# VectorE's share of the exps as fp16 bits: a chain of six passes in place of seven, an offset carried by an added row of Q and K, and new rules for the order of instructions

## The chip, the cores and the metric

One core of a Trainium2 chip. The metric is the device time of one execution in microseconds (us), lower is better. A result is the median of several runs; a verdict calls two kernels the same within 2%. Ratios are the mean time of one kernel's fast runs over that of the other's fast runs of the same rounds, so they are not quite the ratio of the medians quoted beside them.

## The reference

Two independent parts are computed and concatenated. Part A is a spectral filter (a 2-D FFT, a product with complex weights, the inverse FFT) on 2048 x 640. Part B, which the change concerns, is full attention with 32 heads of 20 columns over 2048 positions:

```python
qkv = (x @ wqkv).reshape(B, S, 3, H, Dh).transpose(2, 0, 3, 1, 4)   # H = 32, Dh = 20, S = 2048
scores = einsum("bhqd,bhkd->bhqk", q, k) * Dh ** -0.5
p = softmax(scores, axis=-1)
o = einsum("bhqk,bhkd->bhqd", p, v)
b = o.transpose(0, 2, 1, 3).reshape(B, S, D) @ wo
```

## The kernel before

The kernel cuts attention into 32 units (four blocks of 512 queries by eight groups of four heads). A unit has 64 tiles of 128 keys by 512 queries. TensorE makes the scores of two or three tiles into a half of PSUM. ScalarE takes the exp of that half in one instruction, and TensorE sums the result against V, four heads side by side, into one PSUM bank. A column of ones in V yields the softmax's denominator. Part A's matmuls and evictions are laid between.

ScalarE alone would need longer than the rest, so VectorE computes 238 of the 2048 tiles by itself, two tiles at a time. It turns the score into the bits of a floating-point number and corrects the mantissa with a polynomial:

```python
# first, for each of two tiles, from PSUM (128x512, fp32 -> uint16)
v = score * (1024 * SCALE * LOG2E) + (32 * 1024 + 512)
# then on both together (128x1024, 16 bit), seven passes
sh  = v << 6                                        # step 0  cheap pass
t   = sh * (X_K / 65536) + X_K * X_BETA             # step 1  cheap pass
h   = t * t                                         # step 2  tensor_tensor
t   = t * (X_GAMMA / X_K) + (1 - X_GAMMA * X_BETA)  # step 3  cheap pass
h   = h * t                                         # step 4  tensor_tensor
v   = v + h                                         # step 5  tensor_tensor
v   = v * 0.125 + X_BIAS                            # step 6  cheap pass: now the bits of a bf16
```

No engine's program is written by hand. While the kernel is built, a list scheduler plays it through with a cost per instruction and appends each instruction to its engine's queue when the engine and the inputs are free in that play. On the chip each engine then works its queue strictly in order, and waits by semaphore. So a wrong cost puts instructions in an order in which one engine stands behind another. Three of its rules (cut):

```python
# the weighted sum with V goes when tiles of four heads are ready, or what is left of the unit
if len(pick) < min(least, self.pv_left[u]):       # least = 4
    return False
...
# the unit's end: denominators go out by DMA, come back broadcast over partitions, then normalize
self.dma(rb, src, r=[("rs", u)], w=[("rb",)], ...)
self.dve_urgent.append((self.now + 3600.0, lambda: self.unit_norm(u), ...))
...
# a filler matmul that adds zero, when TensorE's recent share is under WARM_SHARE
if self.share() > self.cfg["WARM_SHARE"]: return False
```

The sums are checked at the end. If they lie outside a certified range, a slow and safe version runs afterwards. With these inputs it never does.

## Time and profile before

| | before |
|---|---|
| median, range | 921.6 us, 921.09 to 927.94 (3 runs) |
| span of the profiled run | 915.7 us |
| ScalarE, VectorE, TensorE busy | 839.7, 815.7, 837.9 us |
| exps on ScalarE: count, busy, idle before them | 724, 828.8 us, 53.4 us |
| VectorE idle before normalize | 15.9 us |
| mean granted TensorE clock | 0.963 of full |

Read "idle before them" as the holes in ScalarE's row of exps. The prediction shows the page's groups and the instructions around two holes. One row of the page is needed besides: the granted TensorE clock in 40 slices of the span, in tenths of full speed.

```profile
PEclk9999999999699999999999998999799999679999
```

Five slices dip (6, 8, 7, 6, 7). Windows of half a microsecond read 0.50 inside the dips and 1.00 outside them, with mixed values only where a dip starts or ends. So the clock has two states here, and a mean of 0.963 means that 2 x 0.037 x 915.7 = 68 us of the span ran at half.

### The profile page before, as it was taken

How to read it: one execution, taken by the hardware profiler on the slowest of the kernel's cores; microseconds unless marked ns; L12 is line 12 of the kernel's file. 1: busy time of each engine (PE TensorE's matmuls, PEld its weight loads, DVE VectorE, ACT ScalarE, POOL GpSimd, SP SyncE). 2: the span in 40 equal slices, each digit the busy share in tenths (PEclk: the TensorE clock that was granted, in tenths of full speed). 3: DMA queues.
4: the chain of work that ended last, by engine and by line, in shares of the span. 5: the costliest groups of instructions: out<-in, count | busy, mean ns of one | idle time of the engine just before them, and what ended most of it. 6: DMA issues, size and time to landing. Idle time of an engine off the chain costs nothing.

```text
span 915.7 us, 16468 instructions
## 1 busy us (share of the span) xinstructions
PE 837.9 (92%) x6731; PEld 291.2 (32%) x6823; DVE 815.7 (89%) x1642; ACT 839.7 (92%) x744; POOL 2.9 (0%) x7
## 2 busy tenths in 40 slices
PE   8999999999899999999999997898899998989986
PEld 4433333333233333322233322223233332223222
DVE  5797799999799998999899999999999898678994
ACT  6898999998799999999999995999799999789993
POOL 1000000000000000000000000000000000000000
PEclk9999999999699999999999998999799999679999
DMA  7430000003200000011001000010010201011100
GB/s 228 87 82 14 2 14 13 14 14 93 73 28 27 13 14 13 14 48 36 13 20 35 13 13 1 13 59 14 1 59 20 78 13 42 1 41 43 42 13 32
DMA packets 31830, 31.85 MB, mean 35 GB/s; under 512 B 13444, under 2 KB 26500, under 8 KB 31492
## 3 DMA queue, kind: packets, MB, share of 16 engines
q1 hardware_dynamic: 31748, 30.73, 11.2%
q8 instruction: 55, 0.90, 0.4%
q14 instruction: 27, 0.22, 0.1%
HBM read 24.97 MB, written 5.50 MB: 33 GB/s over the span
## 4 chain that ended last, share of the span: by engine, by line
ACT 52%; PE 21%; DVE 20%; DMA 5%; issue 1%; SPq 0%; ACTq 0%; DVEq 0%
ACT arena L1714 51%; PE ps L1697 6%; DVE arena L227 4%; DMA arena<-rscr 4%; PE ps L1879 4%; DVE arena L1787 3%; DVE arena L1253 2%; PE ps L1331 2%; DVE arena L1828 1%; DVE arena L1835 1%; DVE arena L1832 1%; PE ps L1596 1%; DVE arena L1258 1%; PE ps L1533 1%; PE ps L1583 1%
## 5 line engine op out<-in xcount | busy, mean ns | idle before, releaser
L1714 ACT ACTIVATE arena<-ps 128x1536 bf16<-128x1536 f32 x724 | 828.8, 1276 | 53.4 <-PE ps L1697 28.2
L1697 PE MATMUL ps<-arena 32*128 32x512 bf16 x2048 | 309.3, 394 | 42.4 <-ACT arena L1714 22.5
L1879 PE MATMUL ps<-arena 128*32 128x512 bf16 (+1 forms) x2048 | 208.3, 401 | 5.0 <-DVE arena L1837 2.2
L1787 DVE TENSOR_SCALAR arena<-ps 128x512 uint16<-128x512 f32 x238 | 163.4, 687 | 30.6 <-PE ps L1697 28.4
L227 DVE CAST arena<-ps 128x512 bf16<-128x512 f32 (+4 forms) x248 | 143.7, 580 | 22.6 <-PE ps L1331 6.1
L1697 PEld LDWEIGHTS ps<-arena 32*128 32x128 bf16 x2048 | 74.3, 91 | 247.9 <-ACT arena L1714 180.7
L1879 PEld LDWEIGHTS ps<-arena 128*32 128x32 bf16 (+1 forms) x2048 | 51.3, 92 | 132.4 <-issue 107.6
L1583 PE MATMUL ps<-arena 128*128 128x512 bf16 x244 | 85.3, 397 | 3.5 <-issue 2.4
L1828 DVE TENSOR_TENSOR arena<-arena 128x1024 f16<-128x1024 f16 x119 | 81.8, 687 | 1.1
L1832 DVE TENSOR_TENSOR arena<-arena 128x1024 f16<-128x1024 f16 x119 | 81.9, 688 | 0.9
L1835 DVE TENSOR_TENSOR arena<-arena 128x1024 uint16<-128x1024 uint16 x119 | 81.5, 685 | 0.6
L1826 DVE TENSOR_SCALAR arena<-arena 128x1024 f16<-128x1024 int16 x119 | 50.4, 424 | 0.8
L1830 DVE TENSOR_SCALAR arena<-arena 128x1024 f16<-128x1024 f16 x119 | 50.1, 421 | 0.9
L1824 DVE TENSOR_SCALAR arena<-arena 128x1024 uint16<-128x1024 uint16 x119 | 50.1, 422 | 0.4
L1837 DVE TENSOR_SCALAR arena<-arena 128x1024 uint16<-128x1024 uint16 x119 | 50.1, 421 | 0.4
L1533 PE MATMUL ps<-arena 128*32 128x512 bf16 x640 | 47.8, 381 | 1.2 <-issue 0.5
L1596 PE MATMUL ps<-arena 128*128 128x512 bf16 x145 | 46.5, 396 | 1.5 <-issue 0.8
L1331 PE MATMUL ps<-arena 128*128 128x320 bf16 (+1 forms) x192 | 43.0, 330 | 4.3 <-DVE arena L1787 4.2
L227 DVE COPY arena<-ps 128x1024 bf16<-128x1024 bf16 (+2 forms) x55 | 40.2, 733 | 6.0 <-PE ps L540 4.6
L1583 PEld LDWEIGHTS ps<-arena 128*128 128x128 bf16 x317 | 26.7, 98 | 44.9 <-issue 39.3
L1964 PE MATMUL ps<-arena 128*128 128x320 bf16 x192 | 38.2, 303 | 0.1
L1942 DVE TENSOR_TENSOR arena<-arena 128x512 bf16<-128x512 f32 x31 | 21.4, 689 | 15.9 <-DMA arena<-rscr 15.4
(71 smaller groups left out, 464.3 us busy)
## 6 DMA issues: line engine op xcount, KB each, us to landing
arena<-rscr SPq DMA_DIRECT2D x31, 256.0 KB
arena<-in_B_x_dram SPq DMA_DIRECT2D x4, 640.0 KB, 6.4
arena<-in_A_x_dram SPq DMA_DIRECT2D x4, 640.0 KB, 6.2
out_dram<-arena SPq DMA_DIRECT2D x16, 160.0 KB, 1.8
out_dram<-arena SPq DMA_DIRECT2D x4, 640.0 KB, 3.4
arena<-f_ciCS SPq DMA_DIRECT2D x2, 1024.0 KB, 5.1
arena<-arena SPq DMA_DIRECT2D x124, 2.0 KB, 1.7
arena<-f_cslab SPq DMA_DIRECT2D x2, 768.0 KB, 4.4
```

Source lines behind the costliest of these rows:

```text
L227: return eng.tensor_copy(out, in_)
L1331: return lambda e: e.matmul(o, l, r_, start=s_, stop=e_)
L1533: inst = e.matmul(ps[32 * j:32 * j + 32, bank, :], self.wqkv[:, cbv, c:c + 32], r_, start=st, stop=sp, tile_position=(0, 32 * j))
L1583: self.P.add("pe", lambda e: e.matmul(ps[:, 6, :], z, k[:, 0, 0:512], start=False, stop=False, skip_group_check=True), r=[("KT", 0, 0), (" ...
L1596: return lambda e: e.matmul(o, l, r_, start=st, stop=sp)
L1697: inst = e.matmul(ps[:, bank, :], kt_[32 * j:32 * j + 32, g, kt * 128:(kt + 1) * 128], q[32 * j:32 * j + 32, :], start=True, stop=True, ti ...
L1714: self.P.add("act", lambda e: e.activation(pt, in_, AF.Exp, scale=SCALE), r=[("ps", h + k) for k in range(n)], w=[("PT", i % 4)], name="exp")
L1787: self.P.add("dve", lambda e: e.tensor_scalar(v, in_, 1024.0 * SCALE * LOG2E, 32.0 * 1024 + 512, ALU.mult, ALU.add), r=[("ps", bank)], **( ...
L1828: t = self.x_op(n, two, lambda e: e.tensor_tensor(h16, t16, t16, ALU.mult), [ka], [kb], "x_q")
L1832: t = self.x_op(n, two, lambda e: e.tensor_tensor(h16, h16, t16, ALU.mult), [ka, kb], [kb], "x_h")
L1835: t = self.x_op(n, two, lambda e: e.tensor_tensor(v, v, h16, ALU.add), [kb, kv], [kv], "x_w")
L1879: inst = e.matmul(ps[32 * j:32 * j + m, 6, :], va[:, kt, 21 * h:21 * h + m], pt, start=st, stop=sp, tile_position=(0, 32 * j))
```

## The change

The intent is to drop the last pass. If the added constant makes 15, the exponent bias of fp16, part of the score itself, the first instruction's bits are already those of fp16 and need no rescaling. So a row is added to Q (46.5) and to K (1.0) in the padding of the 32-row tile, which adds 46.5 to every score; 46.5 x 0.2236 = 15 x ln 2. ScalarE takes the same amount off by an immediate bias in its exp. With it come new scheduling rules: normalize is placed 9.0 us after the broadcast's issue, part A's multiplications and strided copies get truer costs, the weighted sum may go with fewer heads when ScalarE is stuck, and several weights change. The core of the diff:

```diff
-  activation(pt, in_, AF.Exp, scale=SCALE)
+  activation(pt, in_, AF.Exp, scale=SCALE, bias=-15.0 / LOG2E)
-  v = tensor_scalar(score, 1024.0 * SCALE * LOG2E, 32.0 * 1024 + 512, ALU.mult, ALU.add)
+  v = tensor_scalar(score, 1024.0 * SCALE * LOG2E, 31743.0, ALU.mult, ALU.min)
   (six passes remain: shift, a line, sh * line, a second line, product, add to v)
-  elif step == 6:
-      t = self.x_op(n, one, lambda e: e.tensor_scalar(v, v, 0.125, X_BIAS, ALU.mult, ALU.add), ...)
   # evictions of Q and K: a plain copy becomes multiply and add by a [128,1] operand each
+  return e.tensor_scalar(out, in_, m, b, ALU.mult, ALU.add)
   # two reductions of the sums per unit become one (cut)
   ...
-  if len(pick) < min(least, self.pv_left[u]):
+  stuck = (next exp's scores are ready, its output buffer isn't free, ScalarE is idle)      # shortened
+  if len(pick) < (1 if stuck else min(least, heads)):
-  self.dve_urgent.append((self.now + 3600.0, ... unit_norm ...))
+  self.dve_urgent.append((self.now + self.cfg["T_RB"], ... unit_norm ...))                  # 9000
-  costs: 1.0417 * ne + 64 (multiply, combine); 0.52 * n (copy); eviction + 40
+  costs: 1.0417 * ne + 124, + 144;             1.0417 * n for the strided copy; eviction + 3 on VectorE
-  T_A=680000.0, WIN=1000.0, T_X=0.0
+  T_A=760000.0, WIN=1400.0, T_X=40000.0, T_RB=9000.0
```

More of the change, by code (lines that the diff above doesn't have):

```diff
@@ L1122, in mkev @@
                         return lambda e, en: copy_on(e, en, o, in_)
-                    ev = [(mkev, 0.833 * n * 128 + 63, 0.52 * n * 128 + 64, [], [dst_key(c, b0 // 8)] + zwr, [])]
+                    ev = [(mkev, 0.833 * n * 128 + 63, (1.0417 if tag == "UT" else 0.52) * n * 128 + 64, [], [dst_key(c, b0 // 8)] + zwr, [])]
                     aft = after[c] if isinstance(after, dict) else after
@@ L1253, in mkev @@
                     return lambda e, en: e.tensor_tensor(t[k], ps[:, bank, 0:ne], w, ALU.mult)
-                return (mkev, 0.0, 1.0417 * ne + 64, kw, [("tmp", k)] + zw("K", 2), [])
+                return (mkev, 0.0, 1.0417 * ne + 124, kw, [("tmp", k)] + zw("K", 2), [])
             def comb(y, k0, k1, op, key, t=t):
@@ L1258, in mkev @@
                     return lambda e, en: e.tensor_tensor(y, t[k0], t[k1], op)
-                return (mkev, 0.0, 1.0417 * ne + 64, [("tmp", k0), ("tmp", k1), zr("K", 2)], [key] + zw("B", 3), [])
+                return (mkev, 0.0, 1.0417 * ne + 144, [("tmp", k0), ("tmp", k1), zr("K", 2)], [key] + zw("B", 3), [])
             for co in range(2):
@@ L1370 @@
 LOG2E = 1.4426950408889634
-X_K, X_BETA, X_GAMMA = 18.8641107, -0.0282624809, 0.224521806
-X_BIAS = 12084.9708
+Y_ROW = 46.5
+X_A, X_B = 0.30457565, 0.07826797
 MODE = 100.0
 SLACK = 200.0
+F16 = mybir.dt.float16
 DMA_NS = 2200.0
@@ L1415, in alloc @@
         self.outB = [a.bf(take(1280), 640) for _ in range(2)]
-        self.rin = a.f32(take(64), 16)
-        self.rc = a.f32(take(64), 16)
+        self.rr = a.f32(take(128), 32)
+        self.rin, self.rc = self.rr[:, 0:16], self.rr[:, 16:32]
+        self.kq = a.f32(take(32), 8)
         self.mm = a.f32(take(256), 64)
         self.cert = a.f32(take(32), 8)
-        self.flagt = a.f32(take(32), 8)
+        self.flagt = self.cert[:, 6:8]
         self.vmx = a.f32(take(64), 16)
@@ L1462, in setup_B @@
         self.dma(self.ident, cBd.ap(), w=[("ident",)], name="ld_ident")
+        kq = np.zeros((128, 8), np.float32)
+        kq[:, 0] = kq[:, 2] = 1.0
+        kq[20::32, 0:4] = (0.0, 1.0, 0.0, Y_ROW)
+        kqd = self.nc.inline_tensor(kq, self.prefix + "kq")
+        self.dma(self.kq, kqd.ap(), w=[("kq",)], name="ld_kq")
         xB = self.B_x[0].rearrange("(t p) c -> p t c", p=128)
@@ L1492, in setup_B, with add_row @@
         self.wpad("act", 0)
+    def add_row(self, e, en, out, in_, c):
+        m, b = self.kq[:, c:c + 1], self.kq[:, c + 1:c + 2]
+        if en == "act":
+            return e.activation(out, in_, AF.Identity, bias=b, scale=m)
+        return e.tensor_scalar(out, in_, m, b, ALU.mult, ALU.add)
     def wpad(self, en, g):
@@ L1539, in mk_jobs_B_static, with mkev @@
                 J.pe = pe
+                def mkev(bank, g=g, kc=kc):
+                    o = self.KT[:, g, kc * 512:(kc + 1) * 512]
+                    return lambda e, en: self.add_row(e, en, o, ps[:, bank, :], 0)
+                J.ev = [(mkev, 490.0, 600.0, [("kq",)], [("KT", g, kc)], [])]
                 J.mode = "c"
@@ L1600, in mkev @@
             o = self.QA[u % 2]
-            in_ = ps[:, bank, :]
-            return lambda e, en: copy_on(e, en, o, in_)
-        ev = [(mkev, 490.0, 598.0, [], [("QA", u % 2)], [])]
+            return lambda e, en: self.add_row(e, en, o, ps[:, bank, :], 2)
+        ev = [(mkev, 490.0, 600.0, [("kq",)], [("QA", u % 2)], [])]
         cond = lambda p: g in self.wq_done and (u < 2 or self.qk_left[u - 2] == 0)
@@ L1713, in try_exp @@
         in_ = self.ps[:, h:h + n, :].rearrange("p b n -> p (b n)")
-        self.P.add("act", lambda e: e.activation(pt, in_, AF.Exp, scale=SCALE),
+        self.P.add("act", lambda e: e.activation(pt, in_, AF.Exp, scale=SCALE, bias=-15.0 / LOG2E),
                    r=[("ps", h + k) for k in range(n)], w=[("PT", i % 4)], name="exp")
@@ L1786, in try_x_first @@
         key = ("xv", n % NXV)
-        self.P.add("dve", lambda e: e.tensor_scalar(v, in_, 1024.0 * SCALE * LOG2E, 32.0 * 1024 + 512, ALU.mult, ALU.add),
+        self.P.add("dve", lambda e: e.tensor_scalar(v, in_, 1024.0 * SCALE * LOG2E, 31743.0, ALU.mult, ALU.min),
                    r=[("ps", bank)], **({"w": [key]} if k == 0 else {"pw": [key]}), name="x_v")
@@ L1808, in try_x_step @@
             self.x_step(c)
-            if c[1] == 7:
+            if c[1] == 6:
                 self.x_run.remove(c)
@@ L1815, in x_step @@
         n, step, t, pair = c
-        I16, F16 = mybir.dt.int16, mybir.dt.float16
         kv, ka, kb = ("xv", n % NXV), ("xa", n % 2), ("xb", n % 2)
         xv, xa, xb = self.xv[n % NXV], self.xa[n % 2], self.xb[n % 2]
-        v, sh, g = xv.bitcast(U16), xa.bitcast(U16), xa.bitcast(I16)
-        t16, h16 = xa.bitcast(F16), xb.bitcast(F16)
+        v, sh = xv.bitcast(U16), xa.bitcast(U16)
+        a16, b16 = xa.bitcast(F16), xb.bitcast(F16)
         one, two = 336.0, 603.0
@@ L1825, in x_step @@
         elif step == 1:
-            t = self.x_op(n, one, lambda e: e.tensor_scalar(t16, g, X_K / 65536.0, X_K * X_BETA, ALU.mult, ALU.add), [ka], [ka], "x_t")
+            t = self.x_op(n, one, lambda e: e.tensor_scalar(b16, sh, -2.0 ** -24, 2.0 ** -8, ALU.mult, ALU.add), [ka], [kb], "x_l")
         elif step == 2:
-            t = self.x_op(n, two, lambda e: e.tensor_tensor(h16, t16, t16, ALU.mult), [ka], [kb], "x_q")
+            t = self.x_op(n, two, lambda e: e.tensor_tensor(b16, sh, b16, ALU.mult), [ka, kb], [kb], "x_q")
         elif step == 3:
-            t = self.x_op(n, one, lambda e: e.tensor_scalar(t16, t16, X_GAMMA / X_K, 1.0 - X_GAMMA * X_BETA, ALU.mult, ALU.add), [ka], [ka], "x_l")
+            t = self.x_op(n, one, lambda e: e.tensor_scalar(a16, sh, -4.0 * X_B / 65536.0, -4.0 * X_A, ALU.mult, ALU.add), [ka], [ka], "x_l")
         elif step == 4:
-            t = self.x_op(n, two, lambda e: e.tensor_tensor(h16, h16, t16, ALU.mult), [ka, kb], [kb], "x_h")
+            t = self.x_op(n, two, lambda e: e.tensor_tensor(b16, b16, a16, ALU.mult), [ka, kb], [kb], "x_h")
             self.xa_free[n % 2] = t
         elif step == 5:
-            t = self.x_op(n, two, lambda e: e.tensor_tensor(v, v, h16, ALU.add), [kb, kv], [kv], "x_w")
-        elif step == 6:
-            t = self.x_op(n, one, lambda e: e.tensor_scalar(v, v, 0.125, X_BIAS, ALU.mult, ALU.add), [kv], [kv], "x_p")
+            t = self.x_op(n, two, lambda e: e.tensor_tensor(v, v, b16, ALU.add), [kb, kv], [kv], "x_w")
             for k, (u, kt, j) in enumerate(pair):
-                self.pv_ready[u].append((t + SLACK, kt, j, xv[:, 512 * k:512 * k + 512], kv))
+                self.pv_ready[u].append((t + SLACK, kt, j, xv.bitcast(F16)[:, 512 * k:512 * k + 512], kv))
             self.at(t + SLACK)
@@ L1860, in try_pv @@
                 break
-        if len(pick) < min(least, self.pv_left[u]):
+        heads = sum(self.pv_cnt.get((u, j), 0) < 16 for j in range(4))
+        i = self.nexp
+        stuck = i < self.nqk and self.qk_t[i] <= self.now and self.pt_free[i % 4] > self.now + 1e9 and self.tf["act"] <= self.now
+        if len(pick) < (1 if stuck else min(least, heads)):
             return False
@@ L1921, in unit_recip @@
         P.add("dve", lambda e: e.reciprocal(rc, rin), r=[("rin",)], w=[("rc",)], name="recip")
-        m0, m1 = self.mm[:, 2 * u:2 * u + 1], self.mm[:, 2 * u + 1:2 * u + 2]
-        P.add("dve", lambda e: e.tensor_reduce(m0, rin, AX.X, ALU.max), r=[("rin",)], pw=[("mm",)], name="smax")
-        P.add("dve", lambda e: e.tensor_reduce(m1, rin, AX.X, ALU.min), r=[("rin",)], pw=[("mm",)], name="smin")
-        t = self.occupy("dve", 400.0)
+        m, both = self.mm[:, 2 * u:2 * u + 2], self.rr.rearrange("p (c e) -> p c e", c=2)
+        P.add("dve", lambda e: e.tensor_reduce(m, both, AX.X, ALU.max), r=[("rin",), ("rc",)], pw=[("mm",)], name="sums")
+        t = self.occupy("dve", 270.0)
         rs = self.rscr[u]
@@ L1934, in d2 @@
             self.dma(rb, src, r=[("rs", u)], w=[("rb",)], stream="rb", name="rb")
-            self.dve_urgent.append((self.now + 3600.0, lambda: self.unit_norm(u), lambda: self.op_left[:u // NG].count(0) == u // NG))
-            self.at(self.now + 3600.0)
+            self.dve_urgent.append((self.now + self.cfg["T_RB"], lambda: self.unit_norm(u), lambda: self.op_left[:u // NG].count(0) == u // NG))
+            self.at(self.now + self.cfg["T_RB"])
         self.at(t, d1)
@@ L2031, in tail_norm @@
         if qb == 3:
-            m0, m1, ball = self.mm[:, 62:63], self.mm[:, 63:64], self.ps[:, 5, :]
-            self.P.add("dve", lambda e: e.tensor_reduce(m0, ball, AX.X, ALU.max), r=[("ps", 5)], pw=[("mm",)], name="smax")
-            self.P.add("dve", lambda e: e.tensor_reduce(m1, ball, AX.X, ALU.min), r=[("ps", 5)], pw=[("mm",)], name="smin")
+            m0, m1, ball, inv = self.mm[:, 62:63], self.mm[:, 63:64], self.ps[:, 5, :], self.rb
+            self.P.add("dve", lambda e: e.tensor_reduce(m0, ball, AX.X, ALU.max), r=[("ps", 5)], pw=[("mm",)], name="sums")
+            self.P.add("dve", lambda e: e.tensor_reduce(m1, inv, AX.X, ALU.max), r=[("rb",)], pw=[("mm",)], name="sums")
     def tail_act(self):
@@ L2141, in try_bg_ev @@
                            r=[("ps", J.bank)] + list(rk), w=wk, pw=pk, name=J.name + ".ev")
-            t = self.occupy(en, sum(x[1 if en == "act" else 2] for x in J.ev) + 40.0)
+            t = self.occupy(en, sum(x[1 if en == "act" else 2] for x in J.ev) + (40.0 if en == "act" else 3.0))
             J.done_p = t
@@ L2305, in emit_flag @@
         ps = self.ps
-        LO, HI = 2.0 ** -8, 2.0 ** 31
-        P.add("dve", lambda e: e.tensor_reduce(c[:, 0:1], mm, AX.X, ALU.max), r=[("mm",)], w=[("c", 0)], name="cmax")
-        P.add("dve", lambda e: e.tensor_reduce(c[:, 1:2], mm, AX.X, ALU.min), r=[("mm",)], w=[("c", 1)], name="cmin")
+        both = mm.rearrange("p (u c) -> p c u", c=2)
+        P.add("dve", lambda e: e.tensor_reduce(c[:, 0:2], both, AX.X, ALU.max), r=[("mm",)], w=[("c", 0)], name="csum")
         P.add("dve", lambda e: e.tensor_reduce(c[:, 2:3], self.vmx, AX.X, ALU.max), r=[("vmx",)], w=[("c", 2)], name="cv")
-        P.add("dve", lambda e: e.tensor_single_scalar(c[:, 3:4], c[:, 0:1], HI, ALU.is_gt), r=[("c", 0)], w=[("c", 3)], name="f0")
-        P.add("dve", lambda e: e.tensor_single_scalar(c[:, 4:5], c[:, 1:2], LO, ALU.is_lt), r=[("c", 1)], w=[("c", 4)], name="f1")
-        P.add("dve", lambda e: e.tensor_single_scalar(c[:, 5:6], c[:, 2:3], 2.0 ** 60, ALU.is_gt), r=[("c", 2)], w=[("c", 5)], name="f2")
+        P.add("dve", lambda e: e.tensor_single_scalar(c[:, 3:4], c[:, 0:1], 65000.0, ALU.is_le), r=[("c", 0)], w=[("c", 3)], name="f0")
+        P.add("dve", lambda e: e.tensor_single_scalar(c[:, 4:5], c[:, 1:2], 2.0 ** -6, ALU.is_le), r=[("c", 0)], w=[("c", 4)], name="f1")
+        P.add("dve", lambda e: e.tensor_single_scalar(c[:, 5:6], c[:, 2:3], 2.0 ** 60, ALU.is_le), r=[("c", 2)], w=[("c", 5)], name="f2")
         o1 = self.ones1
@@ L2315, in emit_flag @@
               r=[("c", 3), ("c", 4), ("c", 5), ("ones1",)], w=[("ps", 7)], name="fsum")
-        P.add("dve", lambda e: e.tensor_reduce(fl[0:1, 1:2], ps[0:1, 7, 0:3], AX.X, ALU.max), r=[("ps", 7)], w=[("fl", 1)], name="fmax")
+        P.add("dve", lambda e: e.tensor_reduce(fl[0:1, 1:2], ps[0:1, 7, 0:3], AX.X, ALU.min), r=[("ps", 7), ("c", 5)], w=[("fl", 1)], name="fmin")
         fi = fl.bitcast(mybir.dt.int32)[0:1, 0:1]
-        self.flag_task = P.add("dve", lambda e: e.tensor_single_scalar(fi, fl[0:1, 1:2], 0.0, ALU.is_gt), r=[("fl", 1)], w=[("fl", 0)], name="flag")
+        self.flag_task = P.add("dve", lambda e: e.tensor_single_scalar(fi, fl[0:1, 1:2], 127.5, ALU.is_lt), r=[("fl", 1)], w=[("fl", 0)], name="flag")
         self.flag = fi
@@ L2341, in bass_concat_heads__spectral_gfnet__softmax_full_mha__prompt_kernel @@
     arena = Arena(nc, 212832 - 64)
-    fast = FK(nc, arena, *args, cfg=dict(LEAD=20, T_A=680000.0, WARM_SHARE=0.45, RUN=2, PVQ=8, WIN=1000.0, T_X=0.0, AHEAD=45e3))
+    fast = FK(nc, arena, *args, cfg=dict(LEAD=20, T_A=760000.0, WARM_SHARE=0.45, RUN=2, PVQ=8, WIN=1400.0, T_X=40000.0, AHEAD=45e3, T_RB=9000.0))
     fast.build()
```

## The prediction

> **What bounds the kernel now.** I read the page's busy line first, then the costliest groups, then ScalarE's own order of time, then a few microseconds around each long hole in it.
>
> ```profile
> PE 837.9 (92%) x6731; PEld 291.2 (32%) x6823; DVE 815.7 (89%) x1642; ACT 839.7 (92%) x744; POOL 2.9 (0%) x7
> ...
> ACT arena L1714 51%; PE ps L1697 6%; DVE arena L227 4%; DMA arena<-rscr 4%; PE ps L1879 4%; DVE arena L1787 3%; DVE arena L1253 2%; PE ps L1331 2%; DVE arena L1828 1%; DVE arena L1835 1%; DVE arena L1832 1%; PE ps L1596 1%; DVE arena L1258 1%; PE ps L1533 1%; PE ps L1583 1%
> ...
> L1714 ACT ACTIVATE arena<-ps 128x1536 bf16<-128x1536 f32 x724 | 828.8, 1276 | 53.4 <-PE ps L1697 28.2
> L1787 DVE TENSOR_SCALAR arena<-ps 128x512 uint16<-128x512 f32 x238 | 163.4, 687 | 30.6 <-PE ps L1697 28.4
> L1828 DVE TENSOR_TENSOR arena<-arena 128x1024 f16<-128x1024 f16 x119 | 81.8, 687 | 1.1
> L1837 DVE TENSOR_SCALAR arena<-arena 128x1024 uint16<-128x1024 uint16 x119 | 50.1, 421 | 0.4
> L1942 DVE TENSOR_TENSOR arena<-arena 128x512 bf16<-128x512 f32 x31 | 21.4, 689 | 15.9 <-DMA arena<-rscr 15.4
> ```
>
> The first row says that three engines are near full, so none can be called the bound by its share. The second, the chain that ended last, is the one that decides: half of it is ScalarE's exps. In the third they are busy 828.8 us of a span of 915.7 and sit idle only 53.4 us before one of their 724 instructions. The first exp starts at 14.27 us and the last ends near 898.7; start and tail are about 31 us together. So the kernel is start + exps + holes + tail, and nothing this change can do is worth more than the holes, unless exps move from ScalarE to VectorE. In ScalarE's order of time the holes, added up by place, are: before 40 us 2.6; 68 to 128 us 6.2; at 211 us 3.5; 234 to 252 us 6.8; 558 to 577 us 10.8; 590 to 657 us 6.6; 774 to 794 us 8.1; 809 to 820 us 4.3; a few more, about 4. These are the lines of three of them, each with the VectorE or TensorE line that I take for its cause:
>
> ```profile
> 563.35 0.68 DVE L227 CAST arena<-ps 128x512 bf16<-128x512 f32 x1
> 563.95 0.42 DVE L1837 TENSOR_SCALAR arena<-arena 128x1024 uint16<-128x1024 uint16 x1
> 564.09 0.12 PEld L1265 LDWEIGHTS ps<-arena 128*128 128x128 bf16 x2 [3.07 <-DVE arena L227]
> ...
> 564.28 0.69 DVE L1828 TENSOR_TENSOR arena<-arena 128x1024 f16<-128x1024 f16 x1
> ...
> 565.17 0.62 PE L1879 MATMUL ps<-arena 128*21 128x512 bf16 x4
> ...
> 567.99 2.36 ACT L1714 ACTIVATE arena<-ps 128x1536 bf16<-128x1536 f32 x2 [9.33 <-PE ps L1879]
> ```
> ```profile
> 773.84 0.69 DVE L1942 TENSOR_TENSOR arena<-arena 128x512 bf16<-128x512 f32 x1 [2.89 <-DMA arena<-rscr]
> 774.45 0.68 DVE L1787 TENSOR_SCALAR arena<-ps 128x512 uint16<-128x512 f32 x1
> 775.05 0.48 DVE L227 CAST arena<-ps 128x320 bf16<-128x320 f32 x1
> 775.19 0.85 PE L1331 MATMUL ps<-arena 128*128 128x320 bf16 x5 [2.30 <-DVE arena L1787]
> ...
> 776.42 2.36 ACT L1714 ACTIVATE arena<-ps 128x1536 bf16<-128x1536 f32 x2 [2.04 <-PE ps L1697]
> ```
> ```profile
> 780.00:810.00 30.00, 27.61 (x168) 8.41 (x171) 20.94 (x44) 24.39 (x21) 0.00 (x0) 0.77 0.10 32
> ```
>
> At 558 us ScalarE stops for 9.33 us because the weighted sum with V (L1879) has not read its output buffers; the sum waits to gather four heads, and the last heads of this unit are still in VectorE's chain of passes, which stands behind part A's multiplications (L1253, L1258): the chain's last pass (L1837) runs at 563.95, the sum of the unit at 565.17, and TensorE itself had stood 3.07 us behind a VectorE copy. At 771 us VectorE itself stops for 2.89 us on a broadcast DMA (L1942), being in order; TensorE, waiting for a bank, stops 2.30 us; and after that pause its granted clock falls (0.77 over 780 to 810 us), scores come late and ScalarE has hole after hole. The same sequence, normalize waiting 3.07 us and then the clock at half, precedes the holes from 234 us. VectorE is thus rarely the bound of a whole stage, but it is what opens most of the holes.
>
> **What the Trainium skill says.** "VectorE: DVE Perf Modes", section on the perf-mode tier table, puts a 16-bit tensor_scalar in SBUF at four elements a cycle and tensor_tensor at two. The trace agrees: 421 against 687 ns for the same 1024 elements. So of the seven passes on a pair of tiles the change deletes one of the cheap ones. "ScalarE: Activation LUTs", What ACT_TABLE_LOAD costs, gives an ACTIVATE with immediate scale and bias 186 ns + 0.833 ns per element, and 93 ns more for each pointer operand. For 1536 elements that is an estimate of 1466 ns; the trace has 1487 by shape (1066 for 1024, where it gives 1039), so the exp of before carries immediates. The added bias is an immediate too and should cost nothing; as a pointer it would have cost 724 x 93 ns = 67 us. "TensorE: Matmul & The Clock Gate", Part 1, says the array falls to half its clock after an idle window of about 3.4 us. The trace shows the half clock after pauses of 2 to 3 us, so roughly in accord.
>
> **The change, part by part.**
> 1. The pass that rescaled the bits (L1837) goes; the fp16 bits are used as they are. Start to start, back to back, such a pass takes 0.33 us (563.95 to 564.28 at the next pass in the trace), less than its 421 ns, since neighbours overlap in the records. 119 x 0.33 = 40 us of VectorE time. The instruction counts of the changed kernel show 119 chains and 238 VectorE tiles as before, hence also 724 exps on ScalarE: no exps move, and ScalarE's 829 us stay.
> 2. In the chain that remains, three cheap passes and three of 1024-element tensor_tensor (one now mixes uint16 with fp16; the last add mixed them before, at 685 ns). No change expected. A chain's own latency falls by one pass and its hand-over, about 0.33 + 0.1 us out of 3.4.
> 3. The row added to Q and K: 64 evictions (32 of K, 32 of Q) become multiply-and-add by a per-partition operand, 62 of them on VectorE. They read 512 fp32 elements from PSUM as L1787 does, 687 ns against 686 for the plain cast: zero, at worst 62 x 0.1 = 6 us. On TensorE nothing: the row lies in the padding of a 32-row tile.
> 4. One reduction for two per unit: 31 x some 0.05 us start to start, 1.5 us.
> 5. Normalize is placed later: 9.0 us after the broadcast is issued in place of 3.6. The transfer takes 5 to 6.4 us in the chain of before. The 15.4 us that VectorE stood idle there should nearly vanish. This I weigh as much as part 1.
> 6. When ScalarE is stuck for want of an output buffer, the weighted sum may go with fewer than four heads. That is aimed at the 9.33 us hole and the 3.5 us one.
> 7. Orders and weights: part A is spread to 760 in place of 680 us, VectorE's exps start after 40 us, and the true cost of part A's multiplications and strided copies is used (the strided copies take 1.14 to 1.24 us in the trace). 51 fewer filler matmuls (266 against 317). Counting instructions per attention unit in both orders, at trace start-to-start times (0.60 us per 512-element fp32 op, 0.33 a cheap pass, 0.60 a 1024-element tensor_tensor, 0.66 a multiplication of part A, 1.12 per mean exp), VectorE's load goes over ScalarE's by 17 us summed over the units before, and by 6 us after; the worst unit (the twentieth) falls from 36.5 against 27.9 us to 25.0 against 25.7.
>
> What this saves of the holes, by place: 558 to 577 us, 8 of 10.8; 211 us, 2.5 of 3.5; 234 to 252 us, 5 of 6.8; 590 to 657 us, 3 of 6.6; 774 to 820 us, 8 of 12.4; 68 to 128 us, 2.5 of 6.2. Sum 29 us. Of it I take back 3 for new holes that any new order brings. Start (one small load more in front of x) and tail: even. 921.6 - 26 = 896 us. The 40 + 15 us that VectorE is freed of are thus worth about half, because ScalarE is full most of the time.
>
> **The rivals.** (a) VectorE is hidden anyway. ScalarE is busy 30.0 of 30.0 us in many of the thirty stretches; if the holes are TensorE's, born of in-order issue and too many small matmuls, then freeing VectorE moves nothing: 915 to 922 us. For it: most holes are ended by L1697, a matmul. Against: the wait in front of that matmul is in most long holes a VectorE result. (b) The clock takes the gain back. A lighter VectorE makes no denser TensorE, and 51 fillers fewer leave more pauses; each spell at half clock cost 4 to 7 us of holes in the trace. Two spells more would make it about 907 us. (c) The bound is fully ScalarE's: nearly all holes go, 921.6 - 45 = 877 us. Against: holes of the start-up and of PE's order remain. (d) A pointer-operand eviction or a mixed-type product runs slower than its like: 119 x 0.6 us would wipe out part 1; about 912 us. (e) The check on sums trips and the slow path runs: more than double. Sums are near 2048 here, far from its limits of 64 and 65000; under 1%.
>
> **Range and chances.** Around 896, rival (b) and (a) pull up, (c) down: 8 in 10 between 881 and 912. The 2% line is 903.2 us. Faster 0.70, same 0.28, slower 0.02.
>
> **What would show it.** VectorE busy near 770 us; exps still 724 at the same 1487 and 1066 ns; the idle time before normalize under 3 us; idle before exps near 27 instead of 53; no hole of over 4 us near part A's multiplications; mean granted clock no lower than 0.963. I am wrong if the exps lengthen, if the idle before exps stays near 50 with TensorE lines in front, or if the half-clock spells move and stay as many.

## The result, and the profile after

876.87 us median (876.3 to 877.65, 4 runs) against 921.35 us (915.52 to 927.94, 4 runs): ratio 0.9516, 95% interval 0.9451 to 0.958. It is faster, as forecast, but by 44.5 us where 26 had been forecast, below the range of 881 to 912.

The rows of the page after that answer to those shown in the prediction (engines; the chain that ended last by engine; the same groups: exps, first instruction of VectorE's chain, a tensor_tensor of it; and the new eviction of Q and K):

```profile
PE 804.7 (92%) x6687; PEld 285.9 (33%) x6772; DVE 785.9 (90%) x1495; ACT 835.2 (95%) x740; POOL 2.9 (0%) x7
...
PEclk9999999999999999999999999999999999999999
...
ACT 55%; DVE 26%; PE 16%; issue 1%; DMA 0%; SPq 0%; ACTq 0%; DVEq 0%
...
L1733 ACT ACTIVATE arena<-ps 128x1536 bf16<-128x1536 f32 x724 | 826.0, 1277 | 18.8 <-PE ps L1716 9.3
...
L1807 DVE TENSOR_SCALAR arena<-ps 128x512 uint16<-128x512 f32 x238 | 163.1, 685 | 21.6 <-PE ps L1716 20.4
...
L1847 DVE TENSOR_TENSOR arena<-arena 128x1024 f16<-128x1024 uint16 x119 | 81.4, 686 | 1.3
...
L1507 DVE TENSOR_SCALAR arena<-ps,arena 128x512 bf16<-128x512 f32 x62 | 50.0, 806 | 14.1 <-PE ps L1548 9.6
```

The exps are the same 724 with the same mean length (1277 ns), so no work left ScalarE. What shrank is the idle time before them, from 53.4 to 18.8 us. The clock row has no dip left (mean 0.996). The broadcast DMA has left the chain that ended last, 0% where it had 4%. Normalize, from the groups by shape, now waits for nothing:

```profile
L1961 DVE TENSOR_TENSOR arena<-arena 128x512 bf16<-128x512 f32 x31 | 21.2, 683 | 0.0
```

The profiled pair differs by 915.7 - 875.8 = 39.9 us. Holes before exps are 34.6 of it; the exps' busy time, a union in which a restart after each hole counts in full, 2.8; ScalarE's other work 1.7. Start and tail are even (first exp at 14.27 and 14.62 us, 17.0 and 16.8 us after the last). The medians differ by 4.6 us more: 3.9 because the profiled run of before was one of its better ones (917.49 us, median 921.35), the rest because the profiled run of after was its slowest (877.65 us, median 876.87).

The largest hole that remains, in ScalarE's order of time (start, length, the idle time before in brackets), is a new one of 3.32 us; the next stretch of 168 exps has none that the view splits off:

```profile
287.82 191.49 ACT L1733 ACTIVATE arena<-ps 128x1536 bf16<-128x1536 f32 x168 [3.32 <-PE ps L1716]
```

### The profile page after: what moved, and what is told of

It is laid out like the page before. It is cut to its first block, busy times and chain, and to the rows that moved or that the text cites. A ratio compares the mean times of both kernels' runs of the same rounds, so it can differ in the third digit from the quotient of the medians.

```text
span 875.8 us, 16211 instructions
## 1 busy us (share of the span) xinstructions
PE 804.7 (92%) x6687; PEld 285.9 (33%) x6772; DVE 785.9 (90%) x1495; ACT 835.2 (95%) x740; POOL 2.9 (0%) x7
## 4 chain that ended last, share of the span: by engine, by line
ACT 55%; DVE 26%; PE 16%; issue 1%; DMA 0%; SPq 0%; ACTq 0%; DVEq 0%
ACT arena L1733 55%; PE ps L1716 5%; DVE arena L227 5%; DVE arena L1807 4%; PE ps L1899 3%; DVE arena L1507 2%; DVE arena L1847 2%; DVE arena L1851 2%; DVE arena L1854 2%; DVE arena L1253 2%; PE ps L1983 1%; DVE arena L2186 1%; DVE arena L1845 1%; DVE arena L1843 1%; DVE arena L1849 1%
## 5 line engine op out<-in xcount | busy, mean ns | idle before, releaser
L1733 ACT ACTIVATE arena<-ps 128x1536 bf16<-128x1536 f32 x724 | 826.0, 1277 | 18.8 <-PE ps L1716 9.3
L1716 PE MATMUL ps<-arena 32*128 32x512 bf16 x2048 | 303.8, 384 | 47.3 <-ACT arena L1733 33.2
L1899 PE MATMUL ps<-arena 128*32 128x512 bf16 (+3 forms) x2048 | 203.1, 390 | 2.9 <-DVE arena L1923 1.7
L227 DVE CAST arena<-ps 128x320 bf16<-128x320 f32 (+4 forms) x190 | 103.7, 546 | 16.7 <-PE ps L1576 10.1
L1847 DVE TENSOR_TENSOR arena<-arena 128x1024 f16<-128x1024 uint16 x119 | 81.4, 686 | 1.3
L1851 DVE TENSOR_TENSOR arena<-arena 128x1024 f16<-128x1024 f16 x119 | 81.6, 685 | 1.2
L1603 PE MATMUL ps<-arena 128*128 128x512 bf16 x205 | 68.6, 387 | 2.5 <-issue 1.4
L1507 DVE TENSOR_SCALAR arena<-ps,arena 128x512 bf16<-128x512 f32 x62 | 50.0, 806 | 14.1 <-PE ps L1548 9.6
L1849 DVE TENSOR_SCALAR arena<-arena 128x1024 f16<-128x1024 uint16 x119 | 50.2, 422 | 1.1
L1845 DVE TENSOR_SCALAR arena<-arena 128x1024 f16<-128x1024 uint16 x119 | 49.9, 421 | 1.1
L1843 DVE TENSOR_SCALAR arena<-arena 128x1024 uint16<-128x1024 uint16 x119 | 50.0, 423 | 0.6
L1548 PE MATMUL ps<-arena 128*32 128x512 bf16 x640 | 47.3, 381 | 1.6 <-DVE arena L1807 0.8
L227 DVE COPY arena<-ps 128x1024 bf16<-128x1024 bf16 (+2 forms) x55 | 40.1, 732 | 9.4 <-PE ps L540 6.8
L1616 PE MATMUL ps<-arena 128*128 128x512 bf16 x143 | 43.2, 383 | 1.7 <-DVE arena L1507 0.6
L1576 PE MATMUL ps<-arena 128*128 128x80 bf16 (+1 forms) x320 | 33.2, 236 | 0.7 <-DVE arena L1807 0.3
```

The source lines that it names most:

```text
L227: return eng.tensor_copy(out, in_)
L1507: return e.tensor_scalar(out, in_, m, b, ALU.mult, ALU.add)
L1603: self.P.add("pe", lambda e: e.matmul(ps[:, 6, :], z, k[:, 0, 0:512], start=False, stop=False, skip_group_check=True), r=[("KT", 0, 0), (" ...
L1716: inst = e.matmul(ps[:, bank, :], kt_[32 * j:32 * j + 32, g, kt * 128:(kt + 1) * 128], q[32 * j:32 * j + 32, :], start=True, stop=True, ti ...
L1733: self.P.add("act", lambda e: e.activation(pt, in_, AF.Exp, scale=SCALE, bias=-15.0 / LOG2E), r=[("ps", h + k) for k in range(n)], w=[("PT ...
L1843: t = self.x_op(n, one, lambda e: e.tensor_single_scalar(sh, v, 6, ALU.logical_shift_left), [kv], [ka], "x_s")
```

## The experiments

Each edit lets the scheduler order everything anew unless it is said to keep the order. That distinction turned out to matter: a rule can't be taken out of the scheduler without moving many instructions, and even the number of exps left to ScalarE then changes. The runs that keep the order change only the named instruction, and all other queues are the same row for row.

| run | edit | median us | ratio to before | exps on ScalarE | holes us | mean clock |
|---|---|---|---|---|---|---|
| before | | 921.35 | 1 | 724 | 53.4 | 0.963 |
| after | | 876.87 | 0.9516 | 724 | 18.8 | 0.996 |
| a_chain_only | new chain, old rules | 901.72 | 0.9799 | 721 | 40.1 | 0.986 |
| b_sched_only | old chain, new rules | 894.76 | 0.9735 | 731 | 28.9 | 0.999 |
| c_before_rb9 | before, normalize at 9.0 us | 907.01 | 0.9854 | 723 | 46.8 | 0.988 |
| d_after_rb36 | after, normalize at 3.6 us | 884.61 | 0.9599 | 729 | 19.1 | 0.989 |
| e_after_nostuck | after, old rule for four heads | 884.15 | 0.9657 | 727 | 23.4 | 0.997 |
| f_after_oldcost | after, old costs | 895.47 | 0.9702 | 726 | 36.5 | 0.981 |
| g_before_warm60 | before, more fillers | 903.18 | 0.9815 | 725 | 36.6 | 0.997 |
| j_before_norbwait | before's order, no wait for the broadcast | 892.65 | 0.9762 | 724 | 31.6 | 0.990 |
| k_after_pluspass | after's order, a seventh pass | 921.34 | 1.0061 | 724 | 53.0 | 0.989 |
| l_after_nofill | after's order, no fillers | 924.56 | 1.0098 | 724 | 60.6 | 0.878 |
| n_before_minuspass | before's order, six passes | 907.75 | 0.9944 (unclear) | 724 | 44.4 | 0.976 |
| o_before_both | before's order, j and n together | 886.92 | 0.9686 | 724 | 32.2 | 0.984 |
| p, q (and q again as s) | retuned | 873.99, 873.37 (874.53) | 0.9544, 0.9537 (0.9495) | 728, 723 | 11.0, 16.0 | 0.999 |

The experiments ran on three chips; before's own fast runs lie between 911.5 and 928 us over all of them, so the ratio, not the median, is what to compare across the table. Holes and clock are those of the one profiled run. On the 2% question: faster for b, d, f, s and r (after again, 0.9514), same for c, and unclear for all others; the 95% intervals reach 0.3 to 1.8 per cent to either side.

### Which half of the change? (a and b)

```diff
 a: after, with   T_A=680000, WIN=1000, T_X=0, T_RB=3600, the old costs, min(least, pv_left)
 b: before, with  T_A=760000, WIN=1400, T_X=40000, normalize + 9000, the new costs, the rule for a stuck ScalarE
```

> The new chain, the added row and the new check, with every rule and weight of the order as before. Theory T (waits and clock: VectorE's in-order wait for the broadcast and its late results pause TensorE, the clock halves, exps come late): the 15 us of idle time before normalize stay, several half-clock spells stay, about 905 us (1 to 2.5% faster than before). Rival P (the deleted pass itself: 40 us of VectorE time): most of the 44 us is here, 885 us or less.

> The old chain of seven passes with all the new rules of order (normalize 9.0 us after the broadcast, true costs, the rule for a stuck ScalarE, the new weights). Theory T: no idle time before normalize, few half-clock spells, about 890 us. Rival P: VectorE is as full as before, about 910 us.

Both halves pay: 2.0% and 2.65%. Multiplied they make 0.9539, and the whole change measured 0.9516. That does not make them separate effects, for a is not the pass alone. Its new order also shortened the wait before normalize from 15.9 to 7.5 us (theory T had said that the wait stays), left three exps fewer on ScalarE (some 3.4 us) and issued 326 fillers in place of 317; by the mean clock, 25 us of it ran at half in place of 68. With all of this, a is worth 0.0201 x 921 = 18.5 us, about half of the 40 us of VectorE time that the deleted pass takes. The rules are worth 24.4 us although b leaves 731 exps on ScalarE, seven more than before. In time theory T (waits and clock) came closer in a (905 forecast, 901.72 measured) and in b (890 forecast, 894.76 measured); rival P (all in the pass) fails in both.

### The wait for the broadcast (c, d, j)

```diff
 c: before   -  self.now + 3600.0        +  self.now + 9000.0
 d: after    -  T_RB=9000.0              +  T_RB=3600.0
 j: before   -  tensor_tensor(o, osb, rb,  ALU.mult), r=[osb, rb]
             +  tensor_tensor(o, osb, osb, ALU.mult), r=[osb]          # wrong result on purpose; same order
```

> Before with one number changed: normalize 9.0 us after the broadcast's issue in place of 3.6. Theory T: idle before normalize under 1 us, the holes near 234 and 774 us and their half-clock spells gone, about 905 us, mean clock over 0.975. Rival P: within 1% of before.

> After with that number put back to 3.6. Theory T: VectorE idles 10 to 15 us before normalize again, half-clock spells come back, 888 to 895 us, mean clock under 0.985. Rival P: within 0.7% of after (under 883 us).

> Before, instruction for instruction in the same order, but normalize multiplies by itself, so it waits for no DMA (a wrong result on purpose). Only the 15.4 us of VectorE's wait go. If that wait opens holes beyond its own length by way of TensorE's clock (theory T): the half-clock spells near 234, 774 and 810 us go, mean clock over 0.975, 900 to 908 us. If the wait is hidden or only moves (rival): within 0.7% of before.

Run j is the clean one. Nothing but VectorE's wait was taken away, 15.4 us by the profile, and the kernel became 22 us faster (0.9762), more than theory T had forecast: the wait cost about one and a half times its own length. (Its result was wrong.) The reason is in ScalarE's order of time. In before, four of the holes between 776 and 792 us are

```profile
779.48 2.52 ACT L1714 ACTIVATE arena<-ps 128x1536 bf16<-128x1536 f32 x2 [0.70 <-PE ps L1697]
783.52 2.47 ACT L1714 ACTIVATE arena<-ps 128x1536 bf16<-128x1536 f32 x2 [1.52 <-PE ps L1697]
788.06 2.36 ACT L1714 ACTIVATE arena<-ps 128x1536 bf16<-128x1536 f32 x2 [2.07 <-PE ps L1879]
791.83 1.45 ACT L1714 ACTIVATE arena<-ps 128x1536 bf16<-128x1536 f32 x1 [1.40 <-PE ps L1697]
```

and in j the same place of the program is inside one unbroken stretch of 128 exps, while the hole by part A's multiplications stands as it was:

```profile
558.57 4.62 ACT L1714 ACTIVATE arena<-ps 128x1536 bf16<-128x1536 f32 x4 [9.34 <-PE ps L1879]
...
727.62 146.00 ACT L1714 ACTIVATE arena<-ps 128x1536 bf16<-128x1536 f32 x128 [0.31 <-PE ps L1697]
```

In before, VectorE waits 2.89 us until 773.84, and TensorE waits 2.30 us for VectorE until 775.19 (both lines are in the prediction). Windows of before right after show what follows. Each row has the window and its length, the busy time of TensorE, its weight loads, VectorE, ScalarE and GpSimd, and as the third number from the end the granted clock:

```profile
774.00:776.00 2.00, 0.81 (x9) 0.44 (x9) 2.00 (x4) 0.38 (x1) 0.00 (x0) 1.00 0.00 0
776.00:778.00 2.00, 1.67 (x13) 0.52 (x14) 2.00 (x6) 1.58 (x2) 0.00 (x0) 0.63 0.00 0
778.00:780.00 2.00, 2.00 (x11) 0.45 (x11) 1.42 (x4) 1.30 (x2) 0.00 (x0) 0.50 0.00 0
...
792.00:794.00 2.00, 2.00 (x11) 0.43 (x7) 1.24 (x2) 1.82 (x2) 0.00 (x0) 0.60 0.00 0
794.00:796.00 2.00, 2.00 (x18) 0.61 (x16) 1.11 (x3) 1.84 (x3) 0.00 (x0) 1.00 0.04 3
```

So the clock stood at half for 17 us, from about 776.5 to 793.6, and the holes there are 8.1 us together, against 2.9 us of waiting. The first 2.04 us of them came before the clock fell; how the 22 us of the whole kernel divide between pauses and clock isn't measured. In j the windows from 740 to 860 us all read 1.00: with the wait gone the spell is gone.

Run c has the same wait removed by the scheduler's rule (0.0 us idle before normalize) and gains less, 1.5%. Its new order has a hole of 10.89 us by part A's multiplications and, with the clock at half from about 594 to 611 us, 7.1 us of holes behind it. Its fillers also rose from 317 to 370, so c is not as clean as j. Run d puts only 9.1 us of the wait back and lost 0.8%, less than theory T had forecast (888 to 895 us); five exps more on ScalarE, at 826.0 / 724 = 1.14 us each, may make most of it, so d says little about the wait.

### The clock by itself (g, l)

```diff
 g: before   -  WARM_SHARE=0.45          +  WARM_SHARE=0.60
 l: after    -  self.dummy2()            (no filler; its time stays reserved, so the order stays)
```

> Before with fillers up to a share of 0.60 in place of 0.45 (457 in place of 317), nothing else: VectorE's wait for the broadcast stays. If the half clock by itself made a good part of before's holes: mean clock over 0.985 and 900 to 910 us although VectorE idles 15 us as before. If the pauses cost what they cost whatever the clock: within 1% of before.

> After, same order, without the 242 filler matmuls of the steady part. If the held clock is a part of the gain (theory T): mean clock under 0.95, half-clock spells, 890 to 905 us. If the clock doesn't matter (rival P): 876 us or a little less, TensorE having less to do.

Without fillers (266, the text miscounts them) after takes 924.56 us with TensorE having less to do. The order, VectorE's work and ScalarE's are unchanged. Only the clock row is not:

```profile
PEclk9999999998579999967899899798888965599957
```

A mean of 0.878 is 2 x 0.122 x 927 = 226 us at half clock, against 7 us in after, for 47.7 us, more than the forecast of 890 to 905 us allowed. So after too lives on its fillers. Run g goes the other way: 140 fillers more in before raise the clock to 0.997 and save 1.85%. It isn't fully clean, since the new order also halved the wait before normalize (7.6 us). Before's own runs agree with it without any edit: on one chip three runs were 911.53, 919.75 and 922.79 us at mean clocks of 0.976, 0.968 and 0.961. That would also explain why before scatters by over ten microseconds while after's runs lie within 1.4.

### The rules by part A (e, f)

```diff
 e: after    -  (1 if stuck else min(least, heads))     +  min(least, self.pv_left[u])
 f: after    -  124, 144, 1.0417 for the strided copy, + 3     +  64, 64, 0.52, + 40
```

> After with the old rule for the weighted sum (four heads, or what is left of the unit); the order follows. If the rule for a stuck ScalarE is what removed the 9 us hole: a hole of 4 us or more appears near part A's multiplications, 882 to 888 us. If true costs and the shorter chain did it: within 0.5% of after.

> After with the old, too low costs of part A's multiplications and strided copies and the old surcharge per eviction; everything else as in after. If true costs are a main part of what the rules of order give: holes of over 2 us return by part A's multiplications, 885 us or more. If they matter little beside the wait: under 880 us.

Both orders are slower than after's, by 1.4% of before's time without the rule for a stuck ScalarE and by 1.9% with the old costs; three and two exps more on ScalarE are some 3.4 and 2.3 us of that. In each the hole by part A's multiplications comes back, and it is in b as well, which has both rules but the long chain (from ScalarE's order of time, one fence each for e, f and b):

```profile
531.56 1.02 ACT L1733 ACTIVATE arena<-ps 128x1024 bf16<-128x1024 f32 x1 [4.97 <-PE ps L1899]
```

```profile
562.37 3.85 ACT L1733 ACTIVATE arena<-ps 128x1536 bf16<-128x1536 f32 x3 [7.58 <-PE ps L1899]
```

```profile
539.69 5.59 ACT L1714 ACTIVATE arena<-ps 128x1024 bf16<-128x1024 f32 x5 [8.31 <-PE ps L1882]
```

Of the versions tried here, those with the short chain, the true costs and the rule together have no hole of over 4 us there. But the three are not needed for that: a, with the short chain alone, has no hole of over 2.7 us before an exp, and g, with none of the three, none of over 2.6 us. So this hole hangs on the order as a whole. Which of the three does how much is not settled, since each of these edits also gives another order. In f the clock fell to 0.981 as well.

### The pass by itself (k, n, o)

```diff
 k: after    +  tensor_scalar(v, v, 1.0, 0.0, ALU.mult, ALU.add)      # after step 5, unknown to the scheduler
 n: before   -  step 6 of the chain                                    # its time stays reserved; wrong result on purpose
 o: before   -  step 6, and normalize as in j                          # wrong result on purpose
```

> After, same order, with a seventh pass put back into each chain (multiply by one, add zero, in place), unknown to the order: VectorE +40 us. If the prediction's rate (half) holds: 895 us. If VectorE's time is now nearly on the path: 905 us or more. If it is mostly hidden: under 885 us.

> Before, same order, only the seventh pass taken out of each chain (its bits stay unscaled: a wrong result on purpose). VectorE -40 us. At the prediction's rate of a half: about 898 us (before is near 918). If in a fixed order VectorE's time counts in full, as the run with a pass put back suggests: 880 us or less. If the waits are the main thing: 908 us or more, half-clock spells staying.

> Before, same order, without the seventh pass and without normalize's wait for the DMA (wrong result on purpose). If the two overlap in what they remove: about 882 us. If they add: 870 us or less; the 9 us hole by part A's multiplications should remain, shorter.

The two directions are not mirror images. In after's order 40 us more of VectorE (47.3 by its busy time, 833.2 against 785.9) cost 44.5 us, the outcome for time that is nearly on the path (905 us or more). VectorE then carries the chain that ended last:

```profile
DVE 72%; PE 13%; ACT 13%; issue 2%; ACTq 0%; DVEq 0%
```

In before's order 40 us less of VectorE gave no difference that its interval separates from zero (0.9944, 0.9771 to 1.0117; before had several slow runs in those rounds). In the profile, on another chip, the span fell by 10.3 us and the holes by 9.0, the hole at 552 us stayed at 8.93 us, and 16.4 us of waiting for the broadcast stayed too. The freed time turned into waiting in a queue whose order was made for seven passes. Both j and n together (0.9686) gain less than 1% over j alone (0.9762), 5.7 us by the medians, and their intervals overlap; the 886.92 us lie above the 882 forecast for an overlap. One of its five runs had a 20 us spell at half clock, and that is the profiled one. So in before's own order the missing pass is worth some 6 to 10 us of its 40, not clear of noise, and in after's order an added one costs about its full length (k). What the pass alone is worth in an order made for it is not isolated, since a changes the wait and the clock too.

### A faster version (p, q, s, r)

```diff
 p, q: after -  Q's eviction: tensor_scalar(in_, m, b, mult, add)     +  tensor_scalar(in_, b, None, add)
             -  cost of these evictions 600                            +  720
 p:          +  LEAD=28, PVQ=6, T_A=780000, WARM_SHARE=0.48
 q, s:       +  T_X=20000, WIN=1800, T_RB=8000, RUN=3, AHEAD=35e3, WARM_SHARE=0.48
 r:          after, unchanged
```

> An attempt at a faster version: after with Q's eviction as one add by one pointer in place of multiply and add by two, the scheduler told 720 ns for the row evictions, and weights chosen again (LEAD 28, PVQ 6, T_A 780, fillers up to 0.48). One pointer less: 740 to 770 ns in place of 805 for Q's evictions. Time 868 to 880 us; it has 728 exps on ScalarE in place of 724, so 4 us more of them.

> A second set of weights on the same edits (723 exps, T_X 20, WIN 1800, T_RB 8.0, RUN 3): 866 to 880 us. With 8.0 us some waits of normalize could return; if over 5 us of them, it is slower than after.

> After unchanged, for a comparison on one chip with the next: within 0.5% of 877 us.

> The second set of weights again, beside after on the same chip: 873 us, 0.3 to 0.5% under after.

On one chip and in the same rounds, after took 876.6 us (875.64 to 877.05) and the retuned version 874.53 us (873.96 to 874.82). The four runs of each don't overlap. It is faster by 2.1 us, a quarter of a per cent (0.3 to 0.5 had been forecast). Both results are correct. The evictions, from the groups by shape in p (K's with two operands, then Q's with one):

```profile
L1507 DVE TENSOR_SCALAR arena<-ps,arena 128x512 bf16<-128x512 f32 x31 | 25.0, 807 | 9.0 <-PE ps L1548 8.8
...
L1624 DVE TENSOR_SCALAR arena<-ps,arena 128x512 bf16<-128x512 f32 x31 | 23.1, 745 | 4.6 <-PE ps L1616 4.6
```

p's holes are down to 11.0 us; it pays part of that back with 728 exps. q did without p's extra exps and has more holes instead; its median is 0.6 us lower.

## Why the prediction was right or wrong

**Right: the bound.** Half the chain was ScalarE's exps, they stayed at 724 and the same lengths, and the gain came from the holes before them. Most of the signs it named for itself came: 724 exps, no idle time before normalize (0.0 us), no hole of over 4 us, clock not below 0.963. VectorE's busy time (part 3 below) did not come.

**Near in number, not confirmed as a price: part 1, the pass.** The rate of a half was used for 40 us, hence 20. Run a measured 18.5, but it contains half of the wait's removal and most of the clock's rise. In before's own order the pass gave some 6 to 10 us. So the agreement may be luck.

**Wrong: the step "The 40 + 15 us that VectorE is freed of are thus worth about half", for its second term.** At a half the 15 us of waiting (part 5) would be worth 7 or 8. In the unchanged order, taking just this wait away was worth 22 us, and all rules together (parts 5 to 7) 24.4. The wait is not an amount of VectorE time like the pass. It pauses TensorE (2.30 us at 775 us), the clock then stands at half (17 us), and more holes open. The prediction described this sequence and wrote "this I weigh as much as part 1", then kept 1.8 of the 6.8 us of holes at 234 to 252 and 4.4 of the 12.4 at 774 to 820, as if the spells would get shorter. In j no hole of over half a microsecond is left at either place, and in after the clock row has no dip.

**Mis-sized the same way: the sum of holes by place.** It left 27 us; after has 18.8, including the new hole of 3.32 us. The 3 us taken back for new holes was roughly right in size, the savings were too small, mostly at the two places of the wait: the sum takes 5 + 8 = 13 us off there and leaves 6.2, and after's row of exps has no hole of half a microsecond from 200 to 260 us or after 690. At and behind part A's multiplications it leaves 6.4; after has 5.0 us of holes from 470 to 690 us. Of the 18.5 us between 26 and 44.5, the holes are thus 27.4 - 18.8 = 8.6. ScalarE's own busy time, which was to stay, fell by 2.8 + 1.7 = 4.5. The next point has most of the rest.

**Not in the sum: 4 or 5 us from before's runs.** The sum worked from a profiled run of 917.49 us and subtracted from a median of 921.6. In the later rounds before's times rise as its mean clock falls (911.53 us at 0.976, 927.4 at 0.956), so more time at half clock in the median run is likely, but not shown.

**A reading that does not hold: "the half clock after pauses of 2 to 3 us".** The longest pause of TensorE just before each of the six spells at half clock in before (a seventh lies in the tail) was 1.23, 2.58, 1.13, 0.99, 2.30 and 1.55 us, so it fits two of the six. And the prediction's 67 us for a pointer is an estimate from the figure that it quotes; no run here tried it.

**A small miss: part 3.** The row's evictions were put at zero. They take 806 ns where the plain cast takes 686, so 62 x 0.12 = 7.4 us of VectorE, just over the "worst" of 6. VectorE busy came out at 785.9 us, not near 770. The deleted pass's 40 less these 7.4 come to 32.6, near the fall of 29.8.

**The rivals.** (c), 877 us, is the time that was measured, but not for its reason: 18.8 us of holes remain, and the rest is the busy time of restarts and before's worse runs. (b) had the sign reversed: the clock did not take the gain back, it gave a good part of it, although 51 fillers fewer were issued. Run l shows that its fear was not empty, with all fillers gone the whole gain goes. (a) was wrong. (d) was wrong for the product, since uint16 mixed with fp16 ran at 686 ns, and right for the eviction, at the 7.4 us above.

## What to carry to other kernels

In a kernel of strictly ordered queues, price a wait by what it triggers, not by its length: here a 3 us wait of an engine off the path paused TensorE, the clock then fell to half for 17 us, and removing 15.4 us of such waits was worth about one and a half times as much. Removing 40 us of work from VectorE's queue without making the order again gave 10 us at most by its profile, and adding as much that the order did not know of cost it in full. An edit that makes the order again is never one change: look at the waits, the fillers, the clock and the number of exps before its time is called the price of the edit. When before's runs scatter with the granted clock, size the gain from a profile whose time is near the median, not from the best one.

## What the Trainium skill lacked or had wrong

- "TensorE: Matmul & The Clock Gate", Part 1, has the clock fall to half after an idle window of about 3.4 us and rise after one busy window of about that length. Neither fits before's trace as it stands. Its six spells at half clock before the tail began after pauses of TensorE of 1.23, 2.58, 1.13, 0.99, 2.30 and 1.55 us at most, and lasted 17.1, 6.8, 10.2, 3.4, 17.1 and 10.2 us in windows of 2 us, all near multiples of 3.4. From 778 to 792 us the clock read 0.50 although TensorE was busy 13.78 of the 14 us by the records, which model where a matmul ends. What kept it at half is not shown. (The part also tells of kernels whose clock swings between the two states.)
- The same part puts the penalty of the ramp under 1% of a typical span. It says so of the warm-up, and it is no measure of what the clock can cost later: for this kernel, whose TensorE is busy 92% by the records, dropping 266 fillers cost 5.4% (924.56 against 876.87 us). No page that I read tells of matmuls that add zero to hold the clock in the middle of a kernel.
- "VectorE: DVE Perf Modes", Scalar operands, says that a [P, 1] operand can be read but not what it costs: on 128x512 fp32 from PSUM, 686 ns without (a plain cast; 687 for multiply and add by two immediates, L1787), 745 with one, 806 with two, so some 60 ns each.
